# First pass of the last MLP: token blocks of 768 instead of 512, one set of buffers, and one PSUM pool for both passes

## The chip, the cores and the metric

The kernel runs on one NeuronCore of a Trainium2 chip. The metric is the device time in microseconds (us) of one execution, as the median of several. TensorE is called PE in the profile (PEld is its weight load), VectorE DVE, ScalarE ACT, GpSimd POOL, SyncE SP.

## The reference

Three layers follow one another; all arrays are float32, with 4608 tokens of 512 features.

```python
k_s, q_s = softmax(k, axis=2), softmax(q, axis=-1)      # 8 batches, 8 heads, 576 positions, 64 wide
x = einsum('bhsd,bhse->bhde', k_s, v) applied to q_s    # linear attention, then tokens x 512
logits = x @ w_gate + modality_bias[modality_id]        # 8 experts
e = argmax(logits); out = softmax(logits)[e] * (relu(x @ w1[e]) @ w2[e])
h = out @ w_in                                          # last MLP: (4608, 512) @ (512, 2048)
return maximum(0.01 * h, h) @ w_out                     # (4608, 2048) @ (2048, 512)
```

The change lies in the last MLP: the product with w_in and the leaky relu are its first pass, the product with w_out its second.

## The kernel before, in words

**Order of the work.** Attention comes first, then the experts in slots of 512 tokens (nine always, more under a condition), then the last MLP in two passes: `Hidden` (L737 to L859) and `last_product` (L862 to L987). The program's order is each engine's order: every engine and every DMA queue takes its instructions as the Python code issues them, and a tile's next use waits for the last readers and writers of the same memory.

**Numbers.** Each float32 operand x is split by `split` (L479): ScalarE casts it to a rounded high part (L481), VectorE subtracts to get the low part (L482). A product is high times high, high times low and low times high.

**Seven products.** Both passes multiply 2 x 2 blocks with seven products instead of eight (Winograd's form), in the order `ORDER` = 1, 2, 6, 7, 5, 3, 4. The sums of blocks of x are made on VectorE (`sums`, L786 to L789), the sums of the results during eviction.

**First pass.** The tokens are cut into m blocks of 2 x 256 = 512 (`TB` = 256, nine blocks) and w_in into four quarters q. One (m, q) is called a unit here; there are 36, q inside m. A unit has seven products of 12 matmuls (L801): weights 128 x 128, moving operand 128 x 256, into a PSUM tile `hp` of one bank, of which there are six. After each product stands its eviction:

- product 1: ScalarE copies it to s1 (L828), and triggers the store of the first half of the unit before;
- product 2: ScalarE triggers the store of the second half of the unit before; VectorE adds s1 into the first half of `ht` (L834);
- products 6 and 7: VectorE makes s6 (L836) and s7 (L838);
- product 5: ScalarE copies it to s5 (L840), GpSimd adds twice (L841, L842), ScalarE makes two relus (L843, L844), GpSimd subtracts them (L845): one quarter of `ht` is done this way;
- product 3: VectorE adds (L847), then takes the leaky relu of the first half of `ht` (`leak`, L814, 1024 elements wide);
- product 4: VectorE adds (L850), then the leaky relu of one quarter (L814, 512 wide).

The two halves of `ht` (512 KB each) go to `hd` in DRAM by two stores on ScalarE's queue (L811). `ht`, the s tiles and the tile of x (`xr`) have two sets that alternate. In the last quarter of a block, the split of the next block's operand i (`prep`) is issued after product i and before its eviction. The sums of the next block are issued after the second quarter, the load of x (SyncE, L778) two blocks ahead after the fourth. The weights of q = 0 are loaded among the expert slots, those of q = 1 ahead of the pass, those of q = 2 and 3 in its first two units, all on SyncE's queue.

**Between the passes.** After the last unit of the block before the last, and after those of the last block, `ended` issues on SyncE's queue the load of the second pass's first h and the output weights (2 MB each) for products 1, 2, 6 and 7, into memory of operands no longer needed; `tail` (at product 7 of the last unit) splits the first two operands of the second pass. Then come the weights for 5 and 3, the second load of h, and the weights for 4.

**Second pass.** 18 blocks of 256 tokens, seven products each of 24 matmuls (L960) 128 x 256 wide, into a PSUM tile `yp` of a pool of its own with six buffers. Splits run two products ahead. At product 4 of a block, SyncE loads the h of the block after next (L906, two transfers of 1 MB in runs of 2 KB), and GpSimd scatters the rows of the result (L982).

Of the kernel before, what the change touches and what calls it, by code (L numbers as in the profile page):

```python
# [25 lines left out]
NSLOT = 16  # L26
# [398 lines left out]
def slot_tables(tc, con, ps, cst):  # L425
# [48 lines left out]
    ti = con.tile([128, NSLOT * 3 + 2], I32, name="ti")  # L474
    V.tensor_copy(out=ti[:, 0:NSLOT * 3], in_=r.rearrange("p s f -> p (s f)"))
    V.tensor_copy(out=ti[:, NSLOT * 3:NSLOT * 3 + 2], in_=ci[:, 0, 8:17:8])
    return ti
# [7 lines left out]
def experts(ctx, tc, cst, a, region, xd, dense, did, wops, pre):  # L485
# [5 lines left out]
    ti = slot_tables(tc, ctx.enter_context(tc.tile_pool(name="tab", bufs=1, reuse_waits="tile")), ps, cst)  # L491
# [240 lines left out]
TB = 256  # L732
NA = NT // (2 * TB)
# [3 lines left out]
class Hidden:  # L737


    def __init__(self, tc, dense, hd, wops):  # L740
        self.tc, self.nc, self.dense, self.hd, self.wops = tc, tc.nc, dense, hd, wops
        self.w, self.xh, self.xl, self.xr = {}, {}, {}, [None, None]
        self.cnt = 0

    def early(self, p, pw):
        self.xr[0] = p.tile([128, 4, 2 * TB], F32, name="xr0")
        self.x3 = p.tile([128, 3, 2, 2, TB], F32R, name="x3")
        for n, i in enumerate((1, 2, 6)):
            self.xh[i], self.xl[i] = self.x3[:, n, 0], self.x3[:, n, 1]
        self.w0 = pw.tile([128, 7, 1024], F32R, name="wi0")  # L750
        self.weights(self.w0, 0)

    def late(self, p, p2, ps):
# [4 lines left out]
        self.xt = p.tile([128, 4096], F32, name="xt")  # L758
        self.xr[1] = self.xt[:, 0:2048].rearrange("p (k t) -> p k t", k=4)
        self.t = {i: self.xt[:, 2048 + 512 * n:2560 + 512 * n].rearrange("p (k t) -> p k t", k=2) for n, i in enumerate((4, 5, 6, 7))}  # L760
        for i in (7, 5, 3, 4):
            self.operand(p2, i)
        self.ht = [p2.tile([128, 2, 2, 2, TB], F32, name=f"ht{i}") for i in range(2)]
        self.s = [{n: p2.tile([128, 2, TB], F32, name=f"s{n}{i}") for n in (1, 6, 7, 5)} for i in range(2)]

# [7 lines left out]
    def operand(self, p, i):  # L773
        self.xh[i] = p.tile([128, 2, TB], F32R, name=f"xh{i}")
        self.xl[i] = p.tile([128, 2, TB], F32R, name=f"xl{i}")

    def xload(self, m):
        self.nc.sync.dma_start(out=self.xr[m % 2], in_=self.dense[:, 2 * TB * m:2 * TB * m + 2 * TB].rearrange("(k p) t -> p k t", p=128))  # L778

    def block(self, m, i, j):  # L780
        return self.xr[m % 2][:, 2 * i:2 * i + 2, TB * j:TB * j + TB]

    def sums(self, m):
# [330 lines left out]
```

## Time and profile before

| what | value |
|---|---|
| three runs | 1420.99, 1421.89, 1422.07 us; median 1421.89 |
| the profiled execution's own time | 1421.04 us |
| its span | 1419.2 us |
| PE busy in the span | 1311.5 us (92%) |
| DVE busy | 1047.6 us (74%) |
| ACT busy | 586.8 us (41%) |
| POOL busy | 289.0 us (20%) |
| moved by DMA | 279.57 MB, mean 197 GB/s |

The span is the time from the first to the last instruction that the profiler saw; 1.8 us of the execution lie outside of it. Busy shares are means over stages with different limits. In the rows below, times are us from the span's start unless marked ns; `out<-in` are the program's tile names, a group's `x` its count; the mean of a group is that of one instruction. Matmuls overlap, so the pace of PE is read from the distance of starts, not from an instruction's length. What stands in square brackets is how long the engine had been idle and what released it. The granted clock is a share of PE's full speed.

### The profile page before, as it was taken

What the parts mean: (1) busy time and instruction counts of PE and PEld (TensorE: products, weight loads), DVE (VectorE), ACT (ScalarE), POOL (GpSimd) and SP (SyncE); (2) the same over time, 40 slices, a digit from 0 to 9 for tenths busy, and PEclk for the clock granted to TensorE, in tenths of its full rate; (3) what the DMA queues carried; (4) which work ended last, traced back from release to release, by engine and by line L of the source; (5) the groups of instructions that cost most, each with busy time, mean ns of one, the idle gap of its engine ahead of it and who ended that gap; (6) DMA issues with size and microseconds to landing.
All of it is one profiled execution on the core that took longest, in us unless ns stands there. A gap on an engine that the chain in (4) does not pass through costs nothing.

```text
span 1419.2 us, 23583 instructions
## 1 busy us (share of the span) xinstructions
PE 1311.5 (92%) x9189; PEld 1224.6 (86%) x9189; DVE 1047.6 (74%) x1504; ACT 586.8 (41%) x924; POOL 289.0 (20%) x249
## 2 busy tenths in 40 slices
PE   5987719999999999998999999999989999999998
PEld 5876717778777877787999999999989999999998
DVE  4889846867786777746677777787767777877785
ACT  3545415455545554556223323232333333333342
POOL 0004431101110011001334343434321101111111
PEclk9999869999999999999999999999999999999999
DMA  9763246778777878686933332333595343434330
GB/s 371 284 246 127 76 156 232 259 240 279 259 255 247 275 254 263 194 311 195 407 146 134 135 119 104 136 148 120 233 417 205 122 134 123 149 120 134 119 119 30
DMA packets 146970, 279.57 MB, mean 197 GB/s; under 512 B 18208, under 2 KB 70432, under 8 KB 145952
## 3 DMA queue, kind: packets, MB, share of 16 engines
q1 hardware_dynamic: 122064, 208.46, 43.1%
q10 hardware_dynamic: 17232, 48.48, 8.7%
q0 software_dynamic: 7552, 21.02, 4.1%
q8 instruction: 75, 1.23, 0.4%
q14 instruction: 47, 0.39, 0.1%
HBM read 181.59 MB, written 96.32 MB: 196 GB/s over the span
## 4 chain that ended last, share of the span: by engine, by line
issue 26%; DVE 8%; PE 7%; POOL 6%; DMA 3%; ACT 1%; POOLq 0%; SPq 0%; DVEq 0%
PE hp L801 7%; POOL out L982 3%; DMA wi<-wid 2%; POOL s L841 2%; DVE ht L814 1%; DMA hd<-ht 1%; DVE ht L850 1%; DVE ht L847 1%; DVE s L838 1%; DVE x L482 1%; DVE ht L834 1%; DVE s L836 1%; POOL s L842 1%; DVE xl L482 0%; ACT ht L843 0%
## 5 line engine op out<-in xcount | busy, mean ns | idle before, releaser
L801 PE MATMUL hp<-xh,wi 128*128 128x256 f32 x1152 | 212.8, 281 | 4.2 <-DVE ht L850 2.3
L960 PE MATMUL yp<-wi,x 128*128 128x256 f32 x1152 | 191.2, 283 | 0.6 <-DVE x L482 0.6
L801 PEld LDWEIGHTS hp<-xh,wi 128*128 128x128 f32 x1152 | 179.4, 188 | 6.8 <-DVE ht L850 3.7
L960 PE MATMUL yp<-wi,wi 128*128 128x256 f32 x1200 | 178.2, 283 | 0.3 <-DVE wi L482 0.3
L801 PE MATMUL hp<-x,wi 128*128 128x256 f32 x1296 | 164.5, 286 | 9.2 <-ACTq L708 6.4
L801 PEld LDWEIGHTS hp<-x,wi 128*128 128x128 f32 x1296 | 161.0, 195 | 9.6 <-ACTq L708 6.6
L960 PEld LDWEIGHTS yp<-wi,wi 128*128 128x128 f32 x1200 | 163.5, 192 | 0.5 <-DVE wi L482 0.5
L960 PEld LDWEIGHTS yp<-wi,x 128*128 128x128 f32 x1152 | 161.5, 192 | 0.8 <-DVE x L482 0.8
L801 PE MATMUL hp<-xl,wi 128*128 128x256 f32 x576 | 160.7, 279 | 0.0
L553 POOL DMA_INDIRECT xg<-xd,idi x44 | 55.6, 1264 | 398.6 <-DVE hl L575 331.6
L572 PE MATMUL hp<-xh,w1h 128*128 128x512 f32 (+1 forms) x320 | 122.9, 384 | 11.8 <-DVE hl L575 11.2
L583 PE MATMUL yp<-hh,w2h 128*128 128x512 f32 (+1 forms) x320 | 122.9, 384 | 0.0
L572 PE MATMUL hp<-xl,w1h 128*128 128x512 f32 (+1 forms) x320 | 121.6, 380 | 0.0
L572 PE MATMUL hp<-xh,w1l 128*128 128x512 f32 (+1 forms) x320 | 121.6, 380 | 0.0
L583 PE MATMUL yp<-hl,w2h 128*128 128x512 f32 (+1 forms) x320 | 121.5, 380 | 0.0
L583 PE MATMUL yp<-hh,w2l 128*128 128x512 f32 (+1 forms) x320 | 121.4, 379 | 0.0
L982 POOL DMA_INDIRECT out<-yo,idx x36 | 47.4, 1317 | 315.9 <-DVE idx L976 294.3
L482 DVE TENSOR_TENSOR w1l<-st,w1h 128x1024 fp32r<-128x1024 f32 x44 | 53.8, 1227 | 76.5 <-ACT w1h L481 74.1
L801 PEld LDWEIGHTS hp<-xl,wi 128*128 128x128 f32 x576 | 108.0, 187 | 0.0
L814 DVE SCALAR_TENSOR_TENSOR ht<-ht 128x1024 f32<-128x1024 f32 x72 | 104.9, 1457 | 2.5
L841 POOL TENSOR_TENSOR s<-s,s 128x512 f32<-128x512 f32 x36 | 48.7, 1352 | 209.3 <-DVE s L838 163.8
L843 ACT ACTIVATE ht<-s 128x512 f32<-128x512 f32 x36 | 22.8, 633 | 151.5 <-POOL s L842 147.0
(202 smaller groups left out, 2583.5 us busy)
## 6 DMA issues: line engine op xcount, KB each, us to landing
st<-in_w SPq DMA_DIRECT2D x89, 512.0 KB, 6.5
hd<-ht ACTq DMA_DIRECT2D x72, 512.0 KB, 2.9
xt<-hd SPq DMA_DIRECT2D x18, 1024.0 KB, 5.3
hr<-hd SPq DMA_DIRECT2D x18, 1024.0 KB, 5.2
wi<-wid SPq DMA_DIRECT2D x28, 512.0 KB, 10.3
wi<-wod SPq DMA_DIRECT2D x6, 2048.0 KB, 13.1
v<-in_v SPq DMA_DIRECT2D x16, 650.0 KB, 9.7
k<-in_k SPq DMA_DIRECT2D x16, 576.0 KB, 9.4
```

Source lines behind the costliest of these rows:

```text
L482: nc.vector.tensor_tensor(out=lo, in0=src, in1=hi.bitcast(F32), op=ALU.subtract)
L553: nc.gpsimd.indirect_dma_start(out=xg[:, t], out_offset=None, in_=xd, in_offset=bass.IndirectOffsetOnAxis(ap=idi[:, t:t + 1], axis=0), bou ...
L572: nc.tensor.matmul(hp[:, rows], lhsT=w[:, k, 128 * f:128 * f + 128], rhs=x[:, k, rows], start=(n == 0), stop=(n == 11))
L583: nc.tensor.matmul(yp[:, rows], lhsT=w[:, f, 128 * d:128 * d + 128], rhs=h[:, f, rows], start=(n == 0), stop=(n == 23))
L801: self.nc.tensor.matmul(bank[:, g], lhsT=w[:, h, k, 128 * g:128 * g + 128], rhs=x[:, k], start=(n == 0), stop=(n == 5))
L814: V.scalar_tensor_tensor(out=c, in0=c, scalar=0.01, in1=c, op0=ALU.mult, op1=ALU.max)
L834: V.tensor_tensor(out=h[:, 0, 0], in0=bank, in1=s[1], op=ALU.add)
L836: V.tensor_tensor(out=s[6], in0=bank, in1=s[1], op=ALU.add)
L841: G.tensor_tensor(out=s[6], in0=s[6], in1=s[5], op=ALU.add)
L843: nc.scalar.activation(out=h[:, 1, 1], in_=s[5], func=AF.Relu)
L960: nc.tensor.matmul(bank, lhsT=x[:, k], rhs=w[i][:, h, k], start=(c == 0), stop=(c == 23))
L982: ins = nc.gpsimd.indirect_dma_start(out=out, out_offset=bass.IndirectOffsetOnAxis(ap=idi[s % 2][:, t:t + 1], axis=0), in_=y[:, t], in_off ...
```

## The change

The first pass works on blocks of 2 x 384 = 768 tokens (`TA`; six blocks, 24 units; matmuls 384 wide; all elementwise operations of the pass 768 or 1536 wide). `xr`, `h` and the s tiles have one set each. The PSUM tile of a product has two banks, 384 of 512 columns used in each, and there are four of them. The two middle axes of h change places, and `hd` gets a new layout, so that a store of 768 KB has runs of 6 KB. The first half's store is triggered at product 4 of the same unit, the second's still at product 2 of the next. The load of the next block's x follows the first quarter, the sums the second, in every block. The second pass takes its PSUM tiles from the same pool, four instead of six; its loads of h have runs of 1 KB; its first h and some sums lie in other memory. In the experts, the tables of slots are made in a pool that closes at once, their result in another pool. The diff, cut to its core:

```diff
-def slot_tables(tc, con, ps, cst):
+def slot_tables(tc, con, ps, cst, ti):
...
-    ti = con.tile([128, NSLOT * 3 + 2], I32, name="ti")
...
-    return ti
...
-    ti = slot_tables(tc, ctx.enter_context(tc.tile_pool(name="tab", bufs=1, reuse_waits="tile")), ps, cst)
+    ti = wp.tile([128, NSLOT * 3 + 2], I32, name="ti")
+    with tc.tile_pool(name="tab", bufs=1, reuse_waits="tile") as tab:
+        slot_tables(tc, tab, ps, cst, ti)
...
-TB = 256
-NA = NT // (2 * TB)
+TA, TB = 384, 256
+NA = NT // (2 * TA)
...
     def __init__(self, tc, dense, hd, wops):
...
-        self.w, self.xh, self.xl, self.xr = {}, {}, {}, [None, None]
-        self.cnt = 0
-    def early(self, p, pw):
-        self.xr[0] = p.tile([128, 4, 2 * TB], F32, name="xr0")
-        self.x3 = p.tile([128, 3, 2, 2, TB], F32R, name="x3")
-        for n, i in enumerate((1, 2, 6)):
-            self.xh[i], self.xl[i] = self.x3[:, n, 0], self.x3[:, n, 1]
-        self.w0 = pw.tile([128, 7, 1024], F32R, name="wi0")
+        self.w, self.xh, self.xl = {}, {}, {}
+    def early(self, p):
+        self.xr = p.tile([128, 4, 2 * TA], F32, name="xr")
+        self.x2 = p.tile([128, 2, 2, 2, TA], F32R, name="x2")
+        for n, i in enumerate((1, 2)):
+            self.xh[i], self.xl[i] = self.x2[:, n, 0], self.x2[:, n, 1]
+        self.w0 = p.tile([128, 7, 1024], F32R, name="wi0")
...
     def late(self, p, p2, ps):
...
-        self.xt = p.tile([128, 4096], F32, name="xt")
-        self.xr[1] = self.xt[:, 0:2048].rearrange("p (k t) -> p k t", k=4)
-        self.t = {i: self.xt[:, 2048 + 512 * n:2560 + 512 * n].rearrange("p (k t) -> p k t", k=2) for n, i in enumerate((4, 5, 6, 7))}
-        for i in (7, 5, 3, 4):
-            self.operand(p2, i)
-        self.ht = [p2.tile([128, 2, 2, 2, TB], F32, name=f"ht{i}") for i in range(2)]
-        self.s = [{n: p2.tile([128, 2, TB], F32, name=f"s{n}{i}") for n in (1, 6, 7, 5)} for i in range(2)]
+        self.xt = p.tile([128, 4, 2, TA], F32, name="xt")
+        self.t = {i: self.xt[:, n] for n, i in enumerate((4, 5, 6, 7))}
+        for i in (6, 7, 5, 3, 4):
+            self.xh[i] = p2.tile([128, 2, TA], F32R, name=f"xh{i}")
+            self.xl[i] = p2.tile([128, 2, TA], F32R, name=f"xl{i}")
+        self.h = p2.tile([128, 2, 2, 2, TA], F32, name="h")
+        self.s = {n: p2.tile([128, 2, TA], F32, name=f"s{n}") for n in (1, 6, 7, 5)}
     def weights(self, t, q):
...
     def wload(self, q, i):
...
-    def operand(self, p, i):
-        self.xh[i] = p.tile([128, 2, TB], F32R, name=f"xh{i}")
-        self.xl[i] = p.tile([128, 2, TB], F32R, name=f"xl{i}")
     def xload(self, m):
-        self.nc.sync.dma_start(out=self.xr[m % 2], in_=self.dense[:, 2 * TB * m:2 * TB * m + 2 * TB].rearrange("(k p) t -> p k t", p=128))
-    def block(self, m, i, j):
-        return self.xr[m % 2][:, 2 * i:2 * i + 2, TB * j:TB * j + TB]
-    def sums(self, m):
-        V, t = self.nc.vector, self.t
-        b = lambda i, j: self.block(m, i, j)
+        self.nc.sync.dma_start(out=self.xr, in_=self.dense[:, 2 * TA * m:2 * TA * m + 2 * TA].rearrange("(k p) t -> p k t", p=128))
+    def block(self, i, j):
+        return self.xr[:, 2 * i:2 * i + 2, TA * j:TA * j + TA]
+    def sums(self):
+        V, t, b = self.nc.vector, self.t, self.block
...
-    def prep(self, m, i):
-        src = {1: lambda: self.block(m, 0, 0), 2: lambda: self.block(m, 1, 0), 3: lambda: self.block(m, 1, 1)}.get(i, lambda: self.t[i])()
+    def prep(self, i):
+        src = {1: lambda: self.block(0, 0), 2: lambda: self.block(1, 0), 3: lambda: self.block(1, 1)}.get(i, lambda: self.t[i])()
...
     def product(self, q, i, bank):
...
     def run(self, ended, tail):
...
-        def store(u, f):
-            m, q = units[u]
-            nc.scalar.dma_start(out=self.hd[m, q, f], in_=self.ht[u % 2][:, f].rearrange("p j g t -> p (j g t)"))
+        s, h = self.s, self.h
+        def store(m, q, f):
+            nc.scalar.dma_start(out=self.hd[m, f, :, q], in_=h[:, f].rearrange("p g j t -> p g (j t)"))
         def leak(c):
...
         for u, (m, q) in enumerate(units):
-            s, h = self.s[u % 2], self.ht[u % 2]
             for i in ORDER:
...
-                bank = self.ps.tile([128, 2, TB], F32, tag="h", name="hp", bufs=6)
+                tile_ = self.ps.tile([128, 2, 512], F32, tag="h", name="hp", bufs=4)
+                bank = tile_[:, :, 0:TA]
...
-                    self.prep(m + 1, i)
+                    self.prep(i)
...
                 if i == 1:
...
-                    if u:
-                        store(u - 1, 0)
                 elif i == 2:
                     if u:
-                        store(u - 1, 1)
-                    V.tensor_tensor(out=h[:, 0, 0], in0=bank, in1=s[1], op=ALU.add)
+                        store(*units[u - 1], 1)
+                    V.tensor_tensor(out=h[:, 0, :, 0], in0=bank, in1=s[1], op=ALU.add)
                 elif i == 6:
...
                 elif i == 7:
...
-                    nc.scalar.activation(out=h[:, 1, 1], in_=s[5], func=AF.Relu)
+                    nc.scalar.activation(out=h[:, 1, :, 1], in_=s[5], func=AF.Relu)
...
-                    G.tensor_tensor(out=h[:, 1, 1], in0=h[:, 1, 1], in1=s[5], op=ALU.subtract)
+                    G.tensor_tensor(out=h[:, 1, :, 1], in0=h[:, 1, :, 1], in1=s[5], op=ALU.subtract)
                 elif i == 3:
-                    V.tensor_tensor(out=h[:, 0, 1], in0=bank, in1=s[6], op=ALU.add)
-                    leak(h[:, 0].rearrange("p j g t -> p (j g t)"))
+                    V.tensor_tensor(out=h[:, 0, :, 1], in0=bank, in1=s[6], op=ALU.add)
+                    leak(h[:, 0].rearrange("p g j t -> p (g j t)"))
                 else:
-                    V.tensor_tensor(out=h[:, 1, 0], in0=bank, in1=s[7], op=ALU.add)
-                    leak(h[:, 1, 0])
-            if q == (0 if m == 0 else 1) and m + 1 < NA:
-                self.sums(m + 1)
-            if q == (0 if m == 0 else 3) and m + 2 < NA:
-                self.xload(m + 2)
+                    store(m, q, 0)
+                    V.tensor_tensor(out=h[:, 1, :, 0], in0=bank, in1=s[7], op=ALU.add)
+                    leak(h[:, 1, :, 0])
+            if m + 1 < NA:
+                if q == 0:
+                    self.xload(m + 1)
+                elif q == 1:
+                    self.sums()
...
-        store(u, 0)
-        store(u, 1)
+        store(m, q, 1)
 def last_product(tc, did, hd, wops, out):
...
     def views(hidden, p):
-        w0, w1, x3, xr0 = hidden.w0, hidden.w1, hidden.x3, hidden.xr[0]
+        w0, w1 = hidden.w0, hidden.w1
...
-        hr[0] = hidden.xt.rearrange("p (c t) -> p c t", t=TB)
+        xr, xt = hidden.xr.rearrange("p k t -> p (k t)"), hidden.xt.rearrange("p i k t -> p (i k t)")
+        hr[0] = [t[:, 0:2048].rearrange("p (c t) -> p c t", t=TB) for t in (xr, xt)]
+        S[5], S[6] = half(xr[:, 2048:3072]), half(xt[:, 2048:3072])
...
-        ring.append((half(w0[:, 4]), half(w0[:, 5])))
-        S[5] = p.tile([128, 8, 128], F32, name="S5")
...
-        for n, i in enumerate((6, 7)):
-            S[i] = xr0[:, 2 * n:2 * n + 2].rearrange("p a (b t) -> p (a b) t", t=128)
-        x3 = [x3[:, n].rearrange("p h k t -> p (h k t)") for n in range(3)]
-        ring.append((half(x3[0]), half(x3[1])))
-        ring.append((half(w0[:, 6]), half(x3[2])))
+        x2 = hidden.x2.rearrange("p n h k t -> p (n h k t)")
+        ring.append((half(w0[:, 4]), half(w0[:, 5])))
+        ring.append((half(x2[:, 0:1024]), half(x2[:, 1024:2048])))
+        ring.append((half(w0[:, 6]), half(x2[:, 2048:3072])))
...
     def tiles(p):
...
     def late(p):
-        hr[1] = p.tile([128, 16, TB], F32, name="hr1")
-        S[3] = p.tile([128, 8, 128], F32, name="S3")
+        hr[1] = [p.tile([128, 8, TB], F32, name=f"hr1{i}") for i in range(2)]
+        S[3], S[7] = (p.tile([128, 8, 128], F32, name=f"S{i}") for i in (3, 7))
...
     def wload(i):
...
     def load(s):
-        cs = slice(TB * s, TB * s + TB)
+        m, t0 = divmod(TB * s, 2 * TA)
...
-            nc.sync.dma_start(out=hr[s % 2][:, 8 * f:8 * f + 8].rearrange("p (q g) t -> p q (g t)", q=4),
-                              in_=hd[s // 2, :, f, :, 512 * (s % 2):512 * (s % 2) + 512].rearrange("q p x -> p q x"))
-        nc.sync.dma_start(out=idf[s % 2], in_=did[cs].rearrange("(t p) c -> p t c", p=128))
+            nc.sync.dma_start(out=hr[s % 2][f], in_=hd[m, f, :, :, :, t0:t0 + TB].rearrange("p q g t -> p (q g) t"))
+        nc.sync.dma_start(out=idf[s % 2], in_=did[TB * s:TB * s + TB].rearrange("(t p) c -> p t c", p=128))
     def block(s, i, j):
-        return hr[s % 2][:, 8 * j:8 * j + 8, 128 * i:128 * i + 128]
+        return hr[s % 2][j][:, :, 128 * i:128 * i + 128]
...
-            bank = ps.tile([128, TB], F32, tag="y", name="yp", bufs=6)
+            bank = ps.tile([128, 2, 512], F32, tag="h", name="yp", bufs=4)[:, 0, 0:TB]
...
-    hd = dram.tile([NA, 4, 2, 128, 1024], F32, name="hd")
+    hd = dram.tile([NA, 2, 128, 4, 2, 2 * TA], F32, name="hd")
...
                 def pre():
...
-                    hidden.early(p, p)
+                    hidden.early(p)
...
                     def loads():
...
-                    return loads(), lambda: (hidden.prep(0, 1), hidden.prep(0, 2))
+                    return loads(), lambda: (hidden.prep(1), hidden.prep(2))
...
-                with ExitStack() as hctx:
-                    ps = hctx.enter_context(tc.tile_pool(name="ps_w", bufs=2, space=PSUM, reuse_waits="tile"))
-                    hidden.late(p, hctx.enter_context(tc.tile_pool(name="pa2", bufs=1, reuse_waits="tile")), ps)
+                ps = bctx.enter_context(tc.tile_pool(name="ps_w", bufs=2, space=PSUM, reuse_waits="tile"))
+                with tc.tile_pool(name="pa2", bufs=1, reuse_waits="tile") as p2:
+                    hidden.late(p, p2, ps)
...
                     for i in ORDER:
...
-                    hidden.xload(1)
-                    hidden.sums(0)
+                    hidden.sums()
...
-                        hidden.prep(0, i)
+                        hidden.prep(i)
...
-                run(bctx.enter_context(tc.tile_pool(name="ps_b", bufs=2, space=PSUM, reuse_waits="tile")))
+                run(ps)
...
```

## Rows read from the trace of the kernel before

**Rows 1.** Busy by stretch, both passes: us, busy by engine (x), PEclk, DMA share, GB/s
```profile
669.40:1042.30 372.90, 365.93 (x3024) 362.89 (x3024) 279.29 (x345) 116.80 (x205) 138.03 (x105) 0.99 0.46 178
1071.60:1414.10 342.50, 342.50 (x2863) 342.50 (x2862) 262.39 (x319) 129.07 (x134) 44.68 (x34) 1.00 0.37 121
```

**Rows 2.** The chain that ended last, in pass 1: start, us, what
```profile
846.09 14.50 PE hp L801 x120
...
887.15 14.50 PE hp L801 x120
```

**Rows 3.** Timeline of PE, one unit without a pause: start, us, engine, line, operation, operands, count
```profile
888.62 4.48 PE L801 MATMUL hp<-x,wi 128*128 128x256 f32 x36
...
898.60 1.61 PE L801 MATMUL hp<-x,wi 128*128 128x256 f32 x12
```

**Rows 4.** Timeline of PE in an expert slot, the first and last of 29 matmuls
```profile
566.13 0.39 PE L583 MATMUL yp<-hh,w2h 128*128 128x512 f32 x1
...
572.48 0.39 PE L583 MATMUL yp<-hh,w2l 128*128 128x512 f32 x1
```

**Rows 5.** Groups by form, pass 1: busy us, mean ns | idle before, what ended it
```profile
L845 POOL TENSOR_TENSOR ht<-ht,s 128x512 f32<-128x512 f32 x35 | 45.4, 1296 | 50.4 <-ACT s L844 50.4
...
L847 DVE TENSOR_TENSOR ht<-hp,s 128x512 f32<-128x512 f32 x35 | 24.1, 688 | 42.3 <-POOL s L841 40.8 <-PE hp L801 1.5
...
L843 ACT ACTIVATE ht<-s 128x512 f32<-128x512 f32 x35 | 22.2, 633 | 141.6 <-POOL s L842 137.1 <-DMA hd<-ht 4.5
...
L840 ACT COPY s<-hp 128x512 f32<-128x512 f32 x36 | 21.1, 585 | 94.4 <-PE hp L801 61.9 <-DVE ht L814 32.5
...
L481 ACT CAST xh<-xt 128x512 fp32r<-128x512 f32 x31 | 18.0, 615 | 2.3 <-PE hp L801 2.3
...
L482 DVE TENSOR_TENSOR x<-xt,x 128x1024 fp32r<-128x1024 f32 x1 | 1.2, 1215 | 0.0
...
L481 ACT CAST wi<-xt 128x1024 fp32r<-128x1024 f32 x1 | 1.1, 1052 | 1.3 <-POOL ht L845 1.3
```

**Rows 6.** Timelines of POOL, DVE, PE at a change of block: [idle <-releaser]
```profile
877.81 1.61 POOL L841 TENSOR_TENSOR s<-s,s 128x512 f32<-128x512 f32 x1 [4.90 <-DVE s L838]
...
882.19 1.30 POOL L845 TENSOR_TENSOR ht<-ht,s 128x512 f32<-128x512 f32 x1 [1.40 <-ACT s L844]
...
882.65 1.38 DVE L482 TENSOR_TENSOR xl<-xt,xh 128x512 fp32r<-128x512 f32 x1 [4.39 <-ACT xh L481]
...
887.15 0.38 PE L801 MATMUL hp<-xh,wi 128*128 128x256 f32 x1 [0.38 <-DVE ht L850]
```

**Rows 7.** Timeline of PE, the start of pass 1 and its longest pause
```profile
669.35 6.10 PE L801 MATMUL hp<-x,wi 128*128 128x256 f32 x36 [6.43 <-ACTq L708]
...
703.85 5.94 PE L801 MATMUL hp<-x,wi 128*128 128x256 f32 x36 [2.78 <-DMA wi<-wid]
```

**Rows 8.** Busy time by stretch, behind two pauses of PE
```profile
703.80:706.60 2.80, 2.75 (x13) 2.79 (x14) 1.00 (x1) 0.00 (x0) 0.45 (x1) 0.50 1.02 407
1047.20:1052.20 5.00, 4.85 (x24) 4.88 (x25) 3.48 (x5) 1.26 (x2) 3.33 (x3) 0.55 1.04 439
```

**Rows 9.** Landings of the stores, whole span (tile hd), then DMA issues from 1000 to 1060
```profile
DMA to landing us min/median/max: 2.6/4.6/19.3
...
wi<-wod SPq DMA_DIRECT2D x6, 2048.0 KB, 13.1
hd<-ht ACTq DMA_DIRECT2D x10, 512.0 KB, 11.1
```

**Rows 10.** Timelines of DVE and PE between the passes, then a group by form
```profile
1040.82 0.69 DVE L834 TENSOR_TENSOR ht<-hp,s 128x512 f32<-128x512 f32 x1 [4.78 <-DMA hd<-ht]
...
1047.35 5.05 PE L960 MATMUL yp<-wi 128*128 128x256 f32 x24 [5.08 <-issue]
1052.23 3.04 PE L960 MATMUL yp<-wi,x 128*128 128x256 f32 x24
...
L960 PE MATMUL yp<-wo,wi 128*128 128x256 f32 x240 | 35.3, 280 | 1.1 <-DMA wo<-wod 1.1
```

## The prediction

> **What bounds the kernel now.** I read the busy time by stretch first: it cuts the span into stages with different limits. In pass 1 of the last MLP TensorE is busy 365.9 of 372.9 us at full clock, in pass 2 all of the time [rows 1]. So both passes go at TensorE's pace, and what the change can gain or lose is matmul time and TensorE's pauses. Next, the chain of waits: it returns to the same point every 41.06 us, one block of 512 tokens, four quarters (units) long [rows 2]. Third, TensorE's timeline within one clean unit: 84 matmuls of 256 columns take 898.60 − 888.62 = 9.98 us, 0.1188 each [rows 3]. 36 such units would be 359.3 us; pass 1 is 13.6 longer. Of these, 1.6 is a low clock at the start (36 matmuls in 6.10 us against 4.48), 4.2 one wait of 2.78 us for weights and the low clock behind it (5.94 against 4.48) [rows 7]. The other 7.8 lie at the eight changes of block, about 1.0 each (41.06 − 4 × 9.98 = 1.14 at the one read here).
>
> **1. Matmul pace: −10.9.** 3024 matmuls of 256 columns become 2016 of 384, with the same columns in all. The trace has no 384. In the experts 28 steps of 512 columns take 6.35 us, 0.2268 each [rows 4]. A line through 0.1188 and 0.2268 has a part of 0.0108 us that doesn't depend on the columns; at 384 it gives 0.1728, so 14.52 us a unit, 348.4 for 24. Ends: 3/4 of 0.2268 (0.1701; −16.4) and 1.5 times 0.1188 (0.1782; 0). I take the line, since 384 lies midway.
>
> **2. Start: −4.2.** Weights of the second to fourth quarters still come at the same pace, but each unit lasts 4.5 us longer; by the fourth they have 13 us more, against a wait of 2.78 [rows 7]. The low clock of the very start stays.
>
> **3. Changes of block: +14.7.** In the last quarter of a block the next block's operands are split (cast on ScalarE, low part on VectorE) between evictions, in queue order. From the end of product 5 the chain goes: cast 5, copy of product 5 (L840), three additions on GpSimd (L841, L842, L845) with two relus between the last two (L843, L844), cast 3, low part 3, eviction of product 3 (L847), whose bank the next products want. Low part and GpSimd exclude each other: low part 3 takes 1.38 us and ends 0.54 after L845, and L841 takes 1.61 instead of 1.30 [rows 6]. With six banks this costs about 1.0. After the change there are four: the third product of the next block needs the bank of product 3.
> All these go from 512 to 768 wide. VectorE's low part is 0.69 at 512 and 1.215 at 1024, so 0.95; the cast 0.615 and 1.052, so 0.83; copy 0.80 and relu 0.85 by the same slope [rows 5]. GpSimd shows one width, 1.296 at 512. Its ends are 1.296 (no growth) and 1.94 (in proportion). I take 1.83, in proportion but for a fixed part like those of the other two engines (0.16 to 0.38, giving 1.86 to 1.75), nearest to VectorE's.
> From the end of product 5 at 5/7 of the unit (10.37): 0.2 until the cast starts, 0.83, 0.72 (the copy starts 0.08 early), L841 1.83 and 0.31 of exclusion, L842 1.83, relus 1.70, L845 1.83, rest of low part 3 0.81, L847 0.95, hand-overs 0.3: 11.3, so 21.7. The third product of the next block is due at 14.52 + 2 × 2.07 = 18.7. TensorE stands 3.0 us. A pause of 0.38 leaves the pace alone (the clean unit follows it) [rows 3, 6]; behind one of 2.78 the granted clock was 0.50, behind one of 5.08 0.55 (the 1.2 GHz level) [rows 8], at 1.46 to 2.01 us a time [rows 7, 10]. I take 1.5. It is owed in either case: the fourth product needs the bank of product 4, which comes free after the leak of 1536 elements (1.74 by VectorE's slope), low part 4 and L850 (0.95 each), 3.6 us after the third product starts with its 2.07 of work. At full clock TensorE would wait the same 1.5 there. Five changes of 4.5 make 22.5, instead of 7.8.
>
> **4. One set of h and s: 0 in ordinary units, +2.0 at the end.** The eviction of product 2 (L834) must now wait for the store of the first half of the same tile, one unit before. The leak of that half ends some 16.8 into its unit, the store lands 2.6 to 4.6 later [rows 9], 5 to 7 into the next. L834 is due at 4.2, so VectorE stands up to 2.8 us with the evictions of 6 and 7 queued behind it, but TensorE wants that bank only for its sixth product at 10.4. This cover ends at a landing of 7.0. The second half lands before L843 rewrites it at 15. The store's trigger on ScalarE stands ahead of the next unit's copy (L828), which it holds until the leak ends; at a change of block L834 then has until a landing of 5.0.
> At the end of pass 1 the 2 MB loads of the output weights run beside the stores: median landing 11.1, at most 19.3 [rows 9], and L834 waited 4.78 [rows 10]. Longer units ask for the same bytes more slowly, and the stores' runs grow from 4 KB to 6 KB. I take 7.7, between 4.6 and 11.1: 0.7 in each of three units. Ends 0 and 3 × 12.3 = 37.
>
> **5. Into pass 2: −1.0.** The last unit's evictions and the first splits of pass 2 keep their order. TensorE's pause of 5.08 and its low clock stay [rows 10]: the chain behind L834 has some 3.5 us more of width, the unit above it 4.5 more. The wait of 1.1 for the last weights [rows 10] goes, as their load is queued behind the others while the unit is longer. Ends −1.1 and +3.5.
>
> **6. The rest: 0.** The next block's x is now loaded after the first quarter, a unit of 14.5 us ahead of the sums that read it; on SyncE's queue only block 0 has something behind it, the fourth quarter's weights, which have the 13 us of part 2 in hand. In pass 1 DMA is 0.46 busy [rows 1]; if that cover went, VectorE's sums would be late and with them the splits a unit and a half later. Pass 2 has four buffers for six, and fills one in 2.9 us (24 × 342.5 / 2863) [rows 1], against an eviction of under 0.7 [rows 5]. Its loads in runs of 1 KB are asked for two blocks of 20 us ahead with DMA at 0.37 busy [rows 1]; if that cover went, each late us would count in 16 blocks. Slot tables' memory, the wider first splits and the larger first load lie beside the last expert slot: ends −1.1 and +2.8, the two waits for a load that the trace shows [rows 7, 10].
>
> Sum: −10.9 − 4.2 + 14.7 + 2.0 − 1.0 = +0.6. The profiled execution took 1421.04 us, 0.85 under the median 1421.89; against its own time that is 1421.6, on the median 1422.5. 0.2% (2.8 us) is about what a measurement can tell from no change.
>
> **The rivals.**
> A, faster. The wide operations save more of their fixed parts: matmuls at 0.1701 (−5.5, of which 0.7 comes back as the next block's third product is due earlier), GpSimd at 1.60, near midway to its lower end (three on the chain, −0.7 in each of five changes): −8.3, 1414.2. For it: other engines show a fixed part of a quarter; against: one width of GpSimd is all there is.
> B, slower: the single h. If stores land 1.5 times as late as now, in proportion to their size (6.9 for 4.6), L834 is 1.9 late at each change of block, past its 5.0: 9.5, 1432.0; if they stay at 11.1 at the end of the pass, another 3 × 3.4. For it: landings up to 19.3; against: a lone store lands in 2.6 [rows 9]. It decides from 5.0 us on.
> C, slower: widening saves little a column. At 0.1782, +10.9, less 0.3 at five changes and 0.3 in three late units: +8.5, 1431.0. For it: the 0.2268 is from another stage; against: it is the same operation, and it costs 1.91 times 0.1188, not twice. The Trainium skill ("TensorE: Matmul & The Clock Gate", section Back-to-back issue gap) gives a fixed part of 2.5 ns to a lone matmul: by it the pace would save an estimated 2.5 us in all, and the time would be near C's. The two rows disagree with it, 10.8 ns.
>
> **How the numbers follow.** Forecast 0.47, A 0.28, B 0.18, C 0.07. The forecast's own range is 1418.5 to 1426.5 (GpSimd at 1.75 to 1.94, landings at the end of 4.6 to 11.1 in part): 0.10 of it faster, 0.28 same, 0.09 slower. A: 0.24 faster, 0.04 same. B and C: 0.25 slower. So faster 0.34, same 0.32, slower 0.34. The range 1413.0 to 1432.5 reaches A and C and the smaller form of B, and leaves out less than 2 in 10.
>
> **What would show it.** Right: matmul steps of 0.173, a clean unit of 14.5, pass 1 within 372 to 376 us, a pause of about 3 us before the third product of each block with granted clock near 0.5 behind it, ended by L847 (bank of product 3), GpSimd's additions at 1.83; no pause at the weights. Wrong: pauses in ordinary units ended by a store, steps above 0.176, GpSimd under 1.65, changes of block under 3 or over 6 us, or a pass 2 other than 20.1 us a block.

## The result and the profile after

The changed kernel took 1436.49 us in the median of four runs (1434.37 to 1438.24) against 1421.44 of the kernel before: a ratio of 1.0106, 95% interval 1.0088 to 1.0124. The change made the kernel slower by some 15 us. The forecast was 1422.5, its range ended at 1432.5. The profiled execution took 1437.88 us, its span is 1435.8, 16.6 more than before; that is the difference explained here.

Busy time by stretch, first and second pass of the changed kernel (columns as in [rows 1]):

```profile
668.50:1058.20 389.70, 361.69 (x2016) 356.08 (x2017) 267.24 (x232) 109.74 (x136) 129.98 (x70) 0.98 0.46 175
1078.60:1430.00 351.40, 351.40 (x2935) 351.40 (x2934) 271.14 (x331) 132.23 (x137) 46.49 (x35) 1.00 0.39 124
```

The second pass is as saturated as before, in blocks of 20.11 us. The first pass lasts 389.7 us instead of 372.9, with no more matmul time than before: the loss is pauses and the low clock behind some of them. The chain that ended last shows a whole block of it, from product 5 of a block's last unit to the same point one block on (start, us, what):

```profile
855.28 0.71 issue
856.00 0.81 ACT s L832
856.87 1.94 POOL s L833
858.89 1.86 POOL s L834
860.77 0.85 ACT h L835
861.65 0.85 ACT s L836
862.50 0.73 ACT xh L479
863.29 1.86 issue
865.14 0.96 DVE h L839
866.12 1.77 DVE h L808
867.91 6.71 DMA hd<-h
874.74 0.97 DVE h L826
875.76 44.03 PE hp L795 x252
```

Down to L839 it is the chain that the prediction added up; the piece called issue at 863.29 is low part 3 (L480) on VectorE. Then it goes on: leak of the first half of h (L808), its store, which lands after 6.71 us, and L826, which waits for that landing and frees the bank of product 2. VectorE's timeline has both waits, that for cast 3 and that for the store:

```profile
863.25 1.97 DVE L480 TENSOR_TENSOR xl<-xr,xh 128x768 fp32r<-128x768 f32 x1 [6.15 <-ACT xh L479]
...
874.74 0.96 DVE L826 TENSOR_TENSOR h<-hp,s 128x768 f32<-128x768 f32 x1 [4.13 <-DMA hd<-h]
```

TensorE's timeline at this change of block has three pauses (in brackets the idle time and what ended it):

```profile
866.14 0.45 PE L795 MATMUL hp<-xh,wi 128*128 128x384 f32 x1 [2.58 <-DVE h L839]
869.67 0.45 PE L795 MATMUL hp<-xh,wi 128*128 128x384 f32 x1 [1.18 <-DVE h L843]
875.76 0.45 PE L795 MATMUL hp<-xh,wi 128*128 128x384 f32 x1 [1.65 <-DVE h L826]
```

The first two, before the third and the fourth product, were forecast. The third, before the sixth, was not. The fourth change has the same three. The first two changes have a low clock in place of the second pause. The fifth has no third pause: no block of x is left to load there, and the store lands in 5.37 us beside a 1 MB load of h. What ran beside that store stands in the DMA issues of 864 to 872, against those of an ordinary change of unit, 846 to 852 (`xr<-dense` is the load of x, `hd<-h` the two stores of a unit; KB each, median us to landing):

```profile
xr<-dense SPq DMA_DIRECT2D x1, 1536.0 KB, 7.5
hd<-h ACTq DMA_DIRECT2D x2, 768.0 KB, 6.7
...
hd<-h ACTq DMA_DIRECT2D x2, 768.0 KB, 3.3
```

The load of the block after next's x starts at 865.25, as soon as low part 3 has read xr at 865.2, and the store is triggered at 867.91. In the program the load stands behind the first quarter, but on SyncE's queue nothing stands before it. The Trainium skill ("DMA: Bandwidth & Descriptors", section Queues, rings and completion order) says that each of the 16 DMA engines takes turns, packet by packet, between the queues that have work for it. The trace agrees as far as a landing can tell: 6.7 us instead of 3.3 for a store that runs beside one load.

The same view of the kernel before, at 883 to 889 and at 892 to 898, had shown it. It is not among the rows of the prediction, which went by minimum, median and maximum:

```profile
xt<-dense SPq DMA_DIRECT2D x1, 1024.0 KB, 5.4
hd<-ht ACTq DMA_DIRECT2D x2, 512.0 KB, 5.6
...
hd<-ht ACTq DMA_DIRECT2D x2, 512.0 KB, 2.6
```

Near the end of the pass the chain has the dearest piece of this kind; there the store of 1024.53 was triggered 0.1 us after a 2 MB load, and in front of the sixth product of the last block's third unit TensorE stands:

```profile
1024.53 11.76 DMA hd<-h
1036.41 0.97 DVE h L826
...
1037.42 0.69 PE L795 MATMUL hp<-xh,wi 128*128 128x384 f32 x1 [4.71 <-DVE h L826]
```

Last, the second pass. ScalarE's copy of its first product waits for a store; by the program its target lies in the memory that was h. And the casts behind it on ScalarE wait with it (timelines of ACT and PE):

```profile
1073.33 0.37 ACT L955 COPY v<-yp 128x256 f32<-128x256 f32 x1 [6.92 <-DMA hd<-h]
...
1074.70 0.80 PE L951 MATMUL yp<-wi,wi 128*128 128x256 f32 x2 [4.10 <-ACT wi L479]
```

From the starts of units on TensorE: a clean unit lasts 14.58 us; the units behind the five changes 20.88, 20.56, 20.81, 20.57 and 19.47, so 29.4 us of loss; the first three 16.78, 15.57 and 14.83, 3.4 of loss; the late one 21.55, 7.0. From the last unit to the second block of the second pass 10.4 us are lost, before 10.1.

### The profile page after: what moved, and what is told of

Same layout as the page of the kernel before. It is cut to its first block, busy times and chain, and to the rows that moved or that the text cites. A ratio compares the mean times of both kernels' runs of the same rounds, so it can differ in the third digit from the quotient of the medians.

```text
span 1435.8 us, 21228 instructions
## 1 busy us (share of the span) xinstructions
PE 1307.5 (91%) x8181; PEld 1217.9 (85%) x8181; DVE 1033.3 (72%) x1387; ACT 580.6 (40%) x855; POOL 281.6 (20%) x213
## 4 chain that ended last, share of the span: by engine, by line
issue 24%; PE 15%; POOL 5%; DVE 4%; DMA 3%; ACT 1%; POOLq 0%; DVEq 0%; ACTq 0%
PE hp L795 15%; POOL out L973 3%; DMA hd<-h 3%; POOL s L833 1%; DVE h L808 1%; POOL s L834 1%; DVE h L839 1%; DVE h L826 1%; DVE s L830 0%; ACT h L835 0%; ACT s L832 0%; ACT xh L479 0%; ACT s L836 0%; DVE s L828 0%; DVE x L480 0%
## 5 line engine op out<-in xcount | busy, mean ns | idle before, releaser
L795 PE MATMUL hp<-xh,wi 128*128 128x384 f32 x960 | 256.0, 342 | 28.0 <-DVE h L839 13.4
L795 PE MATMUL hp<-xl,wi 128*128 128x384 f32 x480 | 163.3, 340 | 0.0
L795 PE MATMUL hp<-x,wi 128*128 128x384 f32 x576 | 106.5, 340 | 6.6 <-DVEq L708 6.6
L795 PEld LDWEIGHTS hp<-x,wi 128*128 128x128 f32 x576 | 102.8, 191 | 6.7 <-ACTq L708 6.7
L480 DVE TENSOR_TENSOR w1l<-st,w1h 128x1024 fp32r<-128x1024 f32 x44 | 53.7, 1224 | 75.3 <-ACT w1h L479 70.5
L808 DVE SCALAR_TENSOR_TENSOR h<-h 128x1536 f32<-128x1536 f32 (+1 forms) x48 | 98.7, 2055 | 1.7
L833 POOL TENSOR_TENSOR s<-s,s 128x768 f32<-128x768 f32 x24 | 45.3, 1888 | 237.9 <-DVE s L830 133.1
L795 PEld LDWEIGHTS hp<-xl,wi 128*128 128x128 f32 x480 | 91.8, 191 | 0.0
L572 PEld LDWEIGHTS hp<-xh,w1h 128*128 128x128 f32 x320 | 60.5, 189 | 26.6 <-DVE hl L575 13.8
## 6 DMA issues: line engine op xcount, KB each, us to landing
wi<-wod SPq DMA_DIRECT2D x6, 2048.0 KB, 11.1
```

Source lines behind the costliest of these rows:

```text
L480: nc.vector.tensor_tensor(out=lo, in0=src, in1=hi.bitcast(F32), op=ALU.subtract)
L572: nc.tensor.matmul(hp[:, rows], lhsT=w[:, k, 128 * f:128 * f + 128], rhs=x[:, k, rows], start=(n == 0), stop=(n == 11))
L795: self.nc.tensor.matmul(bank[:, g], lhsT=w[:, h, k, 128 * g:128 * g + 128], rhs=x[:, k], start=(n == 0), stop=(n == 5))
L808: V.scalar_tensor_tensor(out=c, in0=c, scalar=0.01, in1=c, op0=ALU.mult, op1=ALU.max)
L833: G.tensor_tensor(out=s[6], in0=s[6], in1=s[5], op=ALU.add)
```

## The experiments

Each ratio is against the kernel before, timed on the same chip as the experiment.

**e1: the load of x behind the stores.**

```diff
...
                 elif i == 2:
                     if u:
                         store(*units[u - 1], 1)
+                    if q == 0 and 0 < m and m + 1 < NA:
+                        self.xload(m + 1, nc.scalar)
...
-                if q == 0:
-                    self.xload(m + 1)
+                if (m, q) == (0, 0):
+                    self.xload(m + 1, nc.sync)
```

> Edit of the changed kernel: the loads of x for blocks 2 to 5 go from SyncE's queue to ScalarE's, behind the store of the second half at product 2 of the first quarter. Theory (the load of x, 1.5 MB, starts by itself as soon as the last split has read xr, at the change of block, and holds up the store there, on which L826, the eviction of product 2, waits with the single h): the first half's store at four changes of block lands in 3.2 to 3.4 us instead of 6.3 to 6.7, the four pauses of TensorE before the sixth product (1.2 to 1.8 us) go, 5 to 7 us in all, 1430 to 1431.5 us. Rival (a store of 768 KB behind a long chain is late by its own size, whatever runs beside it): landings above 5 us and the pauses stay, 1435 to 1438 us.

Ratio 1.0068 (1.0044 to 1.0093) where the changed kernel has 1.0106: 0.0038 of 1421 us, 5.4 us less. The two intervals overlap a little, so the size is known to some 4 us only. VectorE's timeline at the same change of block:

```profile
864.27 1.76 DVE L808 SCALAR_TENSOR_TENSOR h<-h 128x1536 f32<-128x1536 f32 x1
...
869.43 0.96 DVE L828 TENSOR_TENSOR h<-hp,s 128x768 f32<-128x768 f32 x1 [0.67 <-DMA hd<-h]
```

L826 (here L828) waits 0.67 us instead of 4.13, no pause over 0.4 us is left before a sixth product at the first four changes, and the units behind the first four changes last 18.9 to 19.4. The theory holds: the store triggered at 866.06 has landed by 869.43, and its own size is not what made it late. In this trace the first four changes cost 6.6 us less than in the changed kernel and the late unit 2.4 less; the fifth change, with no load of x in either kernel, costs 1.6 more, behind a pause of the same length but at a low clock (granted 0.70, then 0.50, in the 8 us from its end).

**e2: the kernel before with four PSUM tiles.** `bufs=6` of the first pass's tile becomes 4.

> Edit of the kernel before: four PSUM tiles of one bank for the first pass instead of six, nothing else. Theory (the pause before the third product of a block comes from the number of tiles: with four, that product waits for L847, behind the relus, cast 3 and low part 3): a pause of 3 to 4.4 us ended by L847 before the third product at each of eight changes of block, with low clock behind, where six tiles cost about 1.0; in all 25 to 40 us more, 1446 to 1461 us. Rival (the pause comes from the wider operations; four tiles are enough at 512): at most 1 us more per change, 1421 to 1429 us.

Ratio 1.0078 (1.0056 to 1.0100), 11 us: between the two. There is a pause, but not the one expected (timelines of PE and DVE):

```profile
805.94 1.70 PE L801 MATMUL hp<-x,wi 128*128 128x256 f32 x12 [1.65 <-ACT s L828]
809.38 0.39 PE L801 MATMUL hp<-xh,wi 128*128 128x256 f32 x1 [0.33 <-DVE ht L850]
...
806.19 0.68 DVE L847 TENSOR_TENSOR ht<-hp,s 128x512 f32<-128x512 f32 x1
```

The third product takes the tile of the new block's first product, which L828 frees, and not that of product 3, which L847 frees 1.0 us later, when the third product already runs. L828 stands behind casts 3 and 4 on ScalarE, so it is late by the same queue, but less. That the number of tiles alone makes the long pause is not borne out. Four tiles cost 1.4 us a change at 512 more than six.

**e3: the relus behind the splits.** In the changed kernel; `relus` holds the three lines taken out:

```diff
...
                 elif i == 5:
...
-                    nc.scalar.activation(out=h[:, 1, :, 1], in_=s[5], func=AF.Relu)
-                    nc.scalar.activation(out=s[5], in_=s[5], func=AF.Relu, scale=-0.01)
-                    G.tensor_tensor(out=h[:, 1, :, 1], in0=h[:, 1, :, 1], in1=s[5], op=ALU.subtract)
+                    if q < 3 or m + 1 == NA:
+                        relus()
...
                 else:
+                    if q == 3 and m + 1 < NA:
+                        relus()
                     store(m, q, 0)
```

> Edit of the changed kernel: in the last quarter of a block the two relus of product 5 and GpSimd's last subtraction are issued behind the splits of operands 3 and 4 instead of ahead of them; same work, same banks. Theory (the pause before the third product is the length of a chain in queue order: cast 3 stands on ScalarE behind two relus that wait for GpSimd): L839 ends some 6 us earlier, the pauses before the third and fourth product (2.6 to 3.2 and 1.2 us) go, and those before the sixth shrink, as the store is triggered earlier; a change of block costs 0 to 1.5 us instead of 4.9 to 6.3, 20 to 28 us less in all, 1408 to 1417 us. Rival (VectorE has more work in the last quarter than a unit is long, 14 us of 14.6 and its exclusions, so order changes little): at least 3 us per change stay, 1424 to 1437 us.

Ratio 0.9900 (0.9881 to 0.9920): 1408.91 us, 14 us faster than the kernel before and some 29 faster than the changed one. In its trace TensorE has no pause over 0.4 us at any change of block; the units behind them last 14.58 to 14.93. VectorE at one:

```profile
847.01 1.42 DVE L480 TENSOR_TENSOR xl<-xr,xh 128x768 fp32r<-128x768 f32 x1 [1.11 <-ACT xh L479]
848.36 0.94 DVE L843 TENSOR_TENSOR h<-hp,s 128x768 f32<-128x768 f32 x1
849.34 2.43 DVE L808 SCALAR_TENSOR_TENSOR h<-h 128x1536 f32<-128x1536 f32 x1
...
857.11 0.96 DVE L831 TENSOR_TENSOR h<-hp,s 128x768 f32<-128x768 f32 x1 [1.94 <-DMA hd<-h]
```

Low part 3 waits 1.11 us for its cast, where it waited 6.15 in the changed kernel, and the eviction of product 3 (L843) follows. The store still meets the load of x: triggered at 851.80, it has landed by 857.1, and L831 (L826 of the changed kernel) waits 1.94 us. But all this comes so early that TensorE does not stand for it. So the rival (too much work on VectorE) falls: the loss at the changes of block comes from the order on ScalarE's queue.

**e5: the output weights behind the stores.** The loads of weights 1, 2, 6 and 7 go to ScalarE's queue, at product 2 of the next unit.

> Edit of the changed kernel: the loads of the output weights for products 1, 2, 6 and 7 of the second pass go from SyncE's queue, where they start at the end of a unit, to ScalarE's, behind the store of the second half at product 2 of the next unit. Theory (at the end of the first pass TensorE's pause of 4.9 us and the low clock behind it, 7 us in one unit, come from a store of 768 KB that runs beside a 2 MB load and lands in 11.8 us): that store lands under 6 us, the pause goes, 4 to 7 us less, 1429.5 to 1432.5 us. Rival (the bytes to move at the end are what limits; what is not waited for by a store is waited for by the second pass): the pause comes back before the first products of the second pass, within 2 us of the changed kernel, 1434.5 to 1438 us.

Ratio 1.0104 (1.0079 to 1.0130), as the changed kernel: the rival holds. The pause in the late unit is gone, and the second pass stands longer (timelines of PE and ACT):

```profile
1061.94 0.47 PE L953 MATMUL yp<-wi,wi 128*128 128x256 f32 x2 [3.41 <-DMA wi<-wod]
1074.76 0.80 PE L953 MATMUL yp<-wi,wi 128*128 128x256 f32 x2 [8.19 <-ACT wi L479]
...
1073.39 0.37 ACT L957 COPY v<-yp 128x256 f32<-128x256 f32 x1 [12.45 <-DMA hr<-hd]
```

**e10: one load behind one store.** In e3, the load that meets the store; `ended(6)` loads the weights of product 6 on ScalarE's queue, and they are taken out of SyncE's:

```diff
...
                     if u:
                         store(*units[u - 1], 1)
+                    if (m, q) == (NA - 1, 2):
+                        ended(6)
```

> Edit of e3: of the output weights only those for product 6 move to ScalarE's queue, behind the store of the second half at product 2 of the last block's third unit; they start 3.4 us later than in e3, where they start 0.1 us before the store of the first half. Theory (TensorE's pause of 4.3 us in that unit and the low clock behind it, 6.1 us in all, come from this one pair; the rest of the loads has time): the store lands under 6 us, the unit lasts under 16 us, and 3 to 6 us less than e3, ratio 0.986 to 0.988 against the kernel before. Rival (as in e5, what the store doesn't wait for the second pass waits for): within 1.5 us of e3, ratio 0.989 to 0.991.

Ratio 0.9891 (0.9854 to 0.9929), median 1403.63. The interval is too wide to set it apart from e3, but the traces do: the late unit lasts 14.58 us instead of 20.67, L833 (L826 of the changed kernel) waits

```profile
1000.71 0.96 DVE L833 TENSOR_TENSOR h<-hp,s 128x768 f32<-128x768 f32 x1 [0.85 <-DMA hd<-h]
```

0.85 us instead of the 8.54 of e3, and the first block of the second pass lasts 29.74, in e3 29.91. The span is 1400.5 instead of 1406.3. It was this pair alone; e5 moved three loads more than needed.

**e15: e10 again, five rounds.**

> The kernel of e10 again, for its interval: both theories that the runs so far leave (the order of the splits and the one load moved are worth what their traces show) expect 17 to 21 us less than the kernel before, ratio 0.985 to 0.988; if the gain of e10 was a matter of that chip's runs, the ratio is that of e3, 0.990.

Ratio 0.9886 (0.9861 to 0.9911), median 1403.60, 17.2 us less than the kernel before. This is the fastest version of the study; it beats both kernels. Whether its step from e3 is clear in the medians stays open.

**e9: both meetings taken away, the order of the splits as in the change.** The edits of e1 and e10 together in the changed kernel.

> Edit of the changed kernel: the moves of e1 (load of x behind the stores) and of e10 (the weights for product 6 behind the store) together; the order of the splits stays that of the changed kernel. Theory (these two meetings of a store with a load are what the forecast left out, and they add up): the four pauses before the sixth product at a change of block and the pause in the last block's third unit go; a change of block costs 4.3 to 4.8 us, as forecast, and the whole is 9 to 13 us faster than the changed kernel, ratio 0.9985 to 1.004 against the kernel before, where the forecast was 1.0004. Rival (one hides the other, or the second pass waits instead): 6 us or less, ratio above 1.0055.

Ratio 1.0041 (1.0027 to 1.0054), 1426.79 us: 9 us less than the changed kernel (some 3 either way), and 5 above the forecast's ratio. That is the lower end of the 9 to 13 expected, so the two add up for the most part. The late unit is clean (14.58 us). A change of block costs 4.3 to 6.5 us, 5.45 in the mean, not 4.3 to 4.8: no pause over 0.4 us is left before the sixth product at the first four, but at two of them the clock is low for longer (last section). The first block of the second pass loses 1.3 us more than in the changed kernel. So what is left above the forecast does not come from these two meetings.

**e8: e3's edit in the kernel before.**

> Edit of the kernel before: as in e3, in the last quarter of a block the two relus and GpSimd's last subtraction are issued behind the splits of operands 3 and 4. Theory (the order on ScalarE's queue is what a change of block costs, in both kernels; before, 1.1 us at each of seven): the changes cost under 0.3, 6 to 10 us less than the kernel before, some 1414 us; as the changed kernel with the same edit took 1408.9, blocks of 768 are then worth 4 to 7 us by themselves, the rest of their shorter matmul time being lost at the start and the end of the pass. Rival (the order matters only with four PSUM tiles; with six, the 1.1 us have another cause, such as the copy L828 behind the casts): less than 3 us gained.

Ratio 0.9944 (0.9925 to 0.9964), 1414.72 us, 8 us less than the kernel before: the theory holds. Blocks of 768, as e3 has them, are worth the rest, 0.9900 against 0.9944, some 6 us, known to some 4. Every unit from the fifth on lasts 9.98 us. The only pause over 0.4 us that is left in the pass is the wait for weights, which blocks of 768 do away with:

```profile
707.94 5.96 PE L801 MATMUL hp<-x,wi 128*128 128x256 f32 x36 [2.69 <-DMA wi<-wid]
```

**e7: the kernel before with one set of h and s.** `range(2)` of both becomes `range(1)`, used for both.

> Edit of the kernel before: one set of h and of the s tiles instead of two, six PSUM tiles and blocks of 512 as before; the stores stay where they are, so the first half's store is triggered only behind the next unit's first copy. Theory (the single set costs where a store lands beside another load: with six tiles and landings of 2.6 us in ordinary units L834 is late by some 3 us but TensorE wants its bank only seven products later; at the eight changes of block, where the load of x holds the landing at 4.4 to 6 us, and at the end of the pass TensorE waits): clean units stay at 9.98, 3 to 12 us more in all, 1424.5 to 1435 us at 1421.5 to 1423.5 of the kernel before. Rival (the single sets alone cost nothing as long as there are six tiles; only four tiles make a late store visible): within 2 us of the kernel before.

Ratio 1.0374 (1.0355 to 1.0394), 53 us: both were far off. The mechanism is the theory's; its size is not (timeline of PE):

```profile
866.45 6.08 PE L801 MATMUL hp<-x,wi 128*128 128x256 f32 x36 [2.58 <-DVE ht L834]
```

At each change of block L834 waits for the store, and the eighth product from it, the first of the next unit, stands for some 2.6 us; 36 matmuls behind it take 6.08 us instead of 4.48. Two units per block pay: the first lasts 11.8 to 15.1 us instead of some 11.1, the second 11.6 to 12.4 instead of 10.0. The rest is at the end of the pass, where the two units before the last take 16.7 and 13.0 and TensorE stands 11.9 us before the second pass instead of 5.1. So a single set at 512, with these stores, is dearer than all that the change did.

**e11: the second pass's tiles out of the memory of h.** In e3, its result tiles are allocated ahead of the others, and the third split is issued before product 4's eviction in the last unit.

> Edit of e3: the second pass's small result tiles are allocated first, so that they no longer lie in the memory of h, and the split of the third product's operand is issued ahead of the last store's trigger on ScalarE's queue instead of behind it. Theory (the copy of the second pass's first product writes into the memory of h, so ScalarE stands 6 to 7 us until the last store has landed, with the next casts queued behind it; with the cast behind the trigger this makes pauses of 2.3, 0.8, 2.1 to 4.1 and 0.5 to 0.8 us and a low clock): these pauses go, the first block of the second pass lasts under 25 us instead of 29.9, 4 to 9 us less than e3, ratio 0.984 to 0.987 against the kernel before. Rival (the weights or the loads of h come late by as much, behind the stores and the 2 MB loads): the first block stays above 28 us, within 2 us of e3.

Ratio 0.9935 (0.9916 to 0.9954), no gain. The copy of the first product no longer waits for a store, which bears out where its target lay, and the pauses named became shorter. But another came (timeline of PE):

```profile
1037.97 0.50 PE L960 MATMUL yp<-wi,wi 128*128 128x256 f32 x2 [1.18 <-ACT wi L479]
1054.74 4.42 PE L960 MATMUL yp<-wo,wi 128*128 128x256 f32 x24 [6.86 <-DMA wo<-wod]
```

Something has to lie in the memory of h; now it is the target of loads that stand ahead of the last weights on SyncE's queue. That those loads wait for the store is inferred from the order of allocation. A layout in which nothing early lies there was not tried.

## Why the prediction was wrong

Against the span of before the forecast was +0.6 us, measured +16.6.

**1, matmul pace: right.** The line through two rows gave 14.52 us a unit. Two starts of clean units in the changed kernel:

```profile
894.61 4.34 PE L795 MATMUL hp<-x,wi 128*128 128x384 f32 x24
909.19 4.34 PE L795 MATMUL hp<-x,wi 128*128 128x384 f32 x24
```

14.58 us, 0.1736 a matmul; 24 units lose 1.4 us against the line. The Trainium skill ("TensorE: Matmul & The Clock Gate", section Back-to-back issue gap) gives a lone matmul 2.5 ns beside its columns at 2.4 GHz; here the three widths, 0.1188, 0.1736 and 0.2268 us, leave 12 to 13.6 ns, and the measurement decides. The pace is 0.0008 us above the line. Rival C falls, and so does the half of A that hoped for 0.1701.

**2, start: half right.** The wait for weights is gone. But the first three units lose 3.4 instead of 1.6. The low clock of the start costs 2.2 instead of 1.6, and the store of the first unit lands in 7.8 us beside the weights and x, so that L826 is late there too (a pause of 0.72 and 1.0 in all).

**3, changes of block: right as far as it went.** The widths came out close, by groups by form (compare [rows 5]):

```profile
L837 POOL TENSOR_TENSOR h<-h,s 128x768 f32<-128x768 f32 x23 | 42.5, 1847 | 42.2 <-ACT s L836 40.4 <-DMA wi<-wid 1.8
L480 DVE TENSOR_TENSOR xl<-xt,xh 128x768 fp32r<-128x768 f32 x24 | 22.5, 946 | 0.0
L479 ACT CAST xh<-xt 128x768 fp32r<-128x768 f32 x24 | 19.8, 832 | 24.7 <-PE hp L795 17.4 <-DVE xt L781 7.3
L835 ACT ACTIVATE h<-s 128x768 f32<-128x768 f32 x23 | 19.5, 847 | 110.9 <-POOL s L834 110.9
L832 ACT COPY s<-hp 128x768 f32<-128x768 f32 x24 | 19.2, 800 | 116.6 <-PE hp L795 82.4 <-DVE s L828 28.4 <-issue 5.8
```

1.83 was taken for GpSimd and 1.85 measured; rival A falls with it. The pause before the third product was put at 3.0 and is 3.07 once and 2.58 four times; the 1.5 behind it is there, as low clock or as the wait of 1.18 for the bank of product 4. What e3 and e8 add is what the chain was worth: two relus ahead of two casts in one queue, in both kernels.

**4 and 6: the step that failed.** Part 6 said that x is loaded after the first quarter, a unit ahead of the sums, and weighed only whether it comes in time. It starts at the change of block, beside the one store that part 4 allowed 5.0 us there. Rival B had this place, this threshold and a price of 1.9 us a change at a landing of 6.9; landings of 6.3 to 6.7 at four changes cost 1.0 to 1.7 of pause. Its reason, the larger store, is not the one that the runs show: alone the store lands in 3.3, and e1 takes the lateness away by moving the load. B was given 0.18, and "a lone store lands in 2.6" was held against it, when the store that counted was never alone. e1 shows 5.4 us of it. All five changes cost 29.4 instead of 22.5. Not all of this 6.9 is the load: with it out of the way the five cost 24.4 in the trace of e1 and 27.3 in that of e9, and these two differ by how often the clock fell behind like pauses.

**4, the end of the pass: mis-sized.** 2.0 was taken, with a landing of 7.7 in each of three units. One store landed in 11.76, beside a load started 0.1 us earlier, and cost 7.0; the others cost nothing. A value between two medians says nothing about a store that either meets a load or doesn't. e10's trace shows 6.1 of it.

**5, into the second pass: wrong by 1.3 us.** The wait for the last weights went, but 0.3 more is lost in all instead of 1.0 less: the copy of the first product waits 6.92 for a store, in memory that was h.

The differences are 1.4 + 1.8 + 6.9 + 5.0 + 1.3 = 16.4; the pass began 0.8 us earlier (668.53 against 669.35). With the forecast's 0.6 that is 16.2 of the 16.6.

## What to carry to other kernels

Here a load on a queue with nothing ahead of it started as soon as its memory was free (at 865.25, low part 3 ending at 865.2), not where it stands in the program; with a second buffer gone, list what else is on the way at the very moment when the store that must land is triggered. Where an engine's queue has work for a waiting result ahead of work for the next operands, swap them before changing sizes: here that order was worth 8 us before the change and 29 after it. A store or load that "nobody waits for" can be waited for by what is next placed in its memory: here that cost ScalarE's copy 6.92 us.

## What the runs showed of the hardware

The clock behind a pause is not set by the pause's length alone. In the changed kernel, 4 us behind the pauses before the third product of the first three changes (columns as above; the clock is a mean, 0.50 is the 1.2 GHz level and 1.00 the 2.4 GHz level):

```profile
737.60:741.60 4.00, 3.88 (x13) 3.83 (x14) 3.93 (x5) 0.80 (x1) 0.00 (x0) 0.57 0.94 280
801.80:805.80 4.00, 3.79 (x13) 3.28 (x14) 3.94 (x4) 0.80 (x1) 0.00 (x0) 0.63 0.94 286
866.10:870.10 4.00, 2.78 (x14) 2.46 (x15) 3.94 (x4) 0.80 (x1) 0.00 (x0) 1.00 0.96 285
```

The granted clock was 0.57 and 0.63 at the first two changes and 1.00 at the other three, behind pauses of 3.07 at the first and 2.58 at each of the other four. In e9 it fell late at the third and fourth change and stayed low for longer, 0.69 and then 0.50 over the next 4 us; these changes cost 6.4 to 6.5 us, the other three 4.3 to 5.1. What decides it was not found.

A store of 512 KB that runs alone lands in 2.6 us and one of 768 KB in 3.3; beside a load of 1.5 MB the same takes 6.3 to 6.7, beside 2 MB loads 11.8. Here the neighbour weighs more than the size.
